# GEGLU feed-forward on one core: transposing x on TensorE in place of a transposing DMA, with warm-up matmuls and another order of the first loads

## The chip, the core and the metric

The kernel runs on one core of a Trainium2 chip. A core has a matrix engine (TensorE, PE in the profile, with its weight loads listed as PEld), a vector engine (VectorE, DVE), a scalar engine (ScalarE, ACT), GpSimd (POOL) and SyncE (SP), which here only issues transfers. Sixteen DMA engines move data between the main memory (HBM) and the on-chip memory (SBUF). Matmul results land in PSUM, 8 banks of 2 KB in each of 128 partitions. Each engine runs its own list of instructions; they meet at semaphores (`then_inc` raises one, `wait_ge` waits for it).

The metric is the device time of one execution in microseconds (us); the median of the runs counts.

## The reference

```python
B, S, D, F = 32, 32, 1024, 3584          # all bf16
x: (B, S, D)   w_gate, w_up: (D, F)   w_down: (F, D)

def reference(x, w_gate, w_up, w_down):
    return (gelu_tanh(x @ w_gate) * (x @ w_up)) @ w_down
```

With the tokens flattened, x is 1024 x 1024. The first two products are 1024 x 1024 x 3584 each, the third 1024 x 3584 x 1024. A matmul instruction takes 128 x 128 stationary weights and a moving tile of 128 x 512, so the products are 448 instructions each, 1344 in all.

## The kernel before

The contraction of the first two products runs over D, so both operands need D on the partitions. The weights have it so in memory; x has tokens there and must be transposed. The kernel keeps `xT` ([128, 8 chunks of D, 1024 tokens]) in SBUF for the whole run. P = 128, N = D = 1024, TT = DT = 8, TW = 512, TH = 2 halves of the tokens.

```python
    # F in 28 tiles of 128, loaded in groups: sizes 1, 1, 2, then 3 at a time
    NBUF_W = 3                      # weight buffers
    N_EARLY = min(2, NG)            # groups 0 and 1: GpSimd's queue
    N_ACTQ = 1 if NG > N_EARLY else 0   # group 2: ScalarE's queue
    ...
        def w_load(eng, g):         # two transfers, gate and up: rows of nft*128 bf16
            ...
        @block.sync
        def _(sp):
            for dc in range(DT):
                sp.dma_start(
                    out=xT[:, dc, :], in_=xf[:, dc * P : (dc + 1) * P], transpose=True
                ).then_inc(sem_x[dc], 16)
            wd_next = 0
            for g in range(N_EARLY + N_ACTQ, NG):
                slot = g % NBUF_W
                if g >= NBUF_W:
                    sp.wait_ge(sem_mm, last_job_of_group[g - NBUF_W] + 1)
                w_load(sp, g)
                ...                 # and one 1 MB piece of w_down
            ...                     # at the end: the stores of the output
        @block.gpsimd
        def _(pool):
            for g in range(N_EARLY):
                w_load(pool, g)
            ...                     # per job: hT = gu * sigmoid(z)
        @block.tensor
        def _(pe):
            for j, (g, ftl, th) in enumerate(jobs1):      # 56 jobs, 16 matmuls each
                slot = g % NBUF_W
                s = j % 4                                 # four pairs of PSUM banks
                bg = ps[:, 2 * s, 0:TW]
                bu = ps[:, 2 * s + 1, 0:TW]
                if ftl == 0 and th == 0:
                    pe.wait_ge(*w_wait[g])
                if j >= 4:
                    pe.wait_ge(sem_d1, j - 3)
                for wsb, bank in ((wg_sb, bg), (wu_sb, bu)):
                    for dc in range(DT):
                        if j == 0 and wsb is wg_sb:
                            pe.wait_ge(sem_x[dc], 16)
                        last = pe.matmul(bank, lhsT=wsb[...dc...], rhs=xT[:, dc, th * TW : (th + 1) * TW], ...)
                last.then_inc(sem_mm, 1)
            ...                                           # second loop: 16 jobs, 28 matmuls each
```

A job is one F tile for one half of the tokens. Groups 0 and 1 have two jobs each, group 2 has four. Per job ScalarE copies and squares the gate's bank, VectorE makes gate x up and the argument of the sigmoid, ScalarE the sigmoid and GpSimd the final product `hT`. The second loop multiplies `hT` with `w_down`; its results go through `o_sb` to memory.

## Time and profile before

| | us |
|---|---|
| time, median of 6 runs (lowest, highest) | 317.48 (317.3, 318.23) |
| span of the profiled execution | 315.8 |
| PE busy | 295.5 |
| DVE busy | 136.5 |
| ACT busy | 97.4 |
| POOL busy | 74.8 |
| PE idle before the first loop's matmuls, in all | 17.4 |

Times in the profile are microseconds from the start of the span; a line number such as L207 is a line of the kernel. Engine letters with a q (SPq) are the part of an engine that issues transfers. In a group of instructions, `out<-in` names the tensors written and read, and `x8` is how many instructions were merged. What stands in square brackets is the idle time before the instruction and what ended it. The chain of waits follows the work that ended last back to its start. A matmul's own listed duration (379 ns in the steady state) is longer than the distance from one to the next, because they are pipelined; the distance is what counts.

The profile lists these transfers in the first stage: eight transposing loads of x on SyncE's queue, two loads of 512 KB on ScalarE's queue (group 2), and four of 256 KB on GpSimd's (groups 0 and 1). The DMA engines moved 99 GB/s in the first 4 us, then 293, 212, 205 and 194 GB/s in the stages of 4 us up to 20 us.

### The profile page before, as it was taken

To read this page: it belongs to the slowest core of one execution; us is meant where nothing else is said; L and a number is where in the kernel's file an instruction comes from. 1 tells how busy PE (TensorE), PEld (TensorE's weight loads), DVE (VectorE), ACT (ScalarE), POOL (GpSimd) and SP (SyncE) were. 2 spreads that over 40 slices of the span, in tenths; PEclk is the share of its full clock that TensorE was granted. 3 is DMA by queue.
4 is the path that set the end of the run, shared out by engine and by line. 5 is a ranking of instruction groups with operands and counts; after the bars stand their busy time and mean duration, and the time that the engine had idled before them with its cause. 6 is when DMAs were issued, how large, how long until landed. Compare 5 with 4: busy or idle time off the path is not lost.

```text
span 315.8 us, 3313 instructions
## 1 busy us (share of the span) xinstructions
PE 295.5 (94%) x1344; PEld 132.1 (42%) x1344; DVE 136.5 (43%) x120; ACT 97.4 (31%) x178; POOL 74.8 (24%) x64
## 2 busy tenths in 40 slices
PE   0259999999999999999999999999999999999996
PEld 0014444444444444444444444444444444444442
DVE  0002566776676677667667766766000000000000
ACT  1003545445544544554454455444000000000000
POOL 4000433343343334334333433433000000000000
PEclk9999999999999999999999999999999999999999
DMA  7960994508118054090330000000010010001000
GB/s 194 211 126 5 352 309 134 199 3 264 68 47 289 0 173 161 0 312 22 91 110 0 2 0 0 2 0 0 17 35 17 17 35 17 17 17 35 17 17 33
DMA packets 33502, 26.41 MB, mean 84 GB/s; under 512 B 9168, under 2 KB 29648, under 8 KB 33488
## 3 DMA queue, kind: packets, MB, share of 16 engines
q1 hardware_dynamic: 31088, 24.12, 25.5%
q0 software_dynamic: 320, 1.05, 1.5%
q10 hardware_dynamic: 2080, 1.05, 1.3%
q8 instruction: 10, 0.16, 0.2%
q14 instruction: 4, 0.03, 0.0%
HBM read 22.02 MB, written 2.10 MB: 76 GB/s over the span
## 4 chain that ended last, share of the span: by engine, by line
PE 92%; SPq 5%; DMA 1%; DVE 0%; issue 0%
PE ps L207 62%; PE ps L230 31%; SPq L143 5%; DMA xT<-in_x_dram 1%; DVE o_sb L266 0%
## 5 line engine op out<-in xcount | busy, mean ns | idle before, releaser
L207 PE MATMUL ps<-xT,wg_sb 128*128 128x512 bf16 x448 | 109.5, 385 | 17.4 <-DMA wu_sb<-in_w_up_dram 12.0
L207 PE MATMUL ps<-xT,wu_sb 128*128 128x512 bf16 x448 | 107.6, 384 | 0.0
L183 POOL TENSOR_TENSOR hT<-gu_sb,s_sb 128x512 bf16<-128x512 f32 x56 | 70.9, 1267 | 145.9 <-ACT s_sb L295 145.9
L253 DVE SCALAR_TENSOR_TENSOR z_sb<-g_sb 128x512 f32<-128x512 f32 x56 | 97.1, 1733 | 0.0
L230 PE MATMUL ps<-wd_sb,hT 128*128 128x512 bf16 x448 | 96.9, 379 | 0.0
L248 DVE TENSOR_TENSOR gu_sb<-g_sb,ps 128x512 f32<-128x512 f32 x56 | 38.5, 688 | 88.9 <-ACT g_sb L286 88.9
L207 PEld LDWEIGHTS ps<-xT,wg_sb 128*128 128x128 bf16 x448 | 44.2, 99 | 73.6 <-DMA wu_sb<-in_w_up_dram 12.0
L283 ACT ACTIVATE g_sb<-ps 128x512 f32<-128x512 f32 x56 | 33.4, 597 | 124.1 <-PE ps L207 124.1
L207 PEld LDWEIGHTS ps<-xT,wu_sb 128*128 128x128 bf16 x448 | 44.2, 99 | 53.8 <-issue 1.9
L230 PEld LDWEIGHTS ps<-wd_sb,hT 128*128 128x128 bf16 x448 | 43.8, 98 | 52.9
L266 DVE CAST o_sb<-ps 128x512 bf16<-128x512 f32 x8 | 5.5, 692 | 88.4 <-PE ps L230 88.4
L295 ACT ACTIVATE s_sb<-z_sb 128x512 f32<-128x512 f32 x56 | 35.4, 632 | 1.9 <-DVE z_sb L253 1.9
L286 ACT ACTIVATE g_sb<-ps 128x512 f32<-128x512 f32 x56 | 33.1, 591 | 0.0
L310 ACT ACTIVATE o_sb<-ps 128x512 bf16<-128x512 f32 x8 | 4.8, 597 | 82.3 <-PE ps L230 82.3
L133 POOL DMA_DIRECT2D wg_sb<-in_w_gate_dram x2 | 1.9, 966 | 0.8 <-POOLq L328 0.8
L283 ACT ACT_TABLE_LOAD x1 | 1.3, 1283 | 1.8 <-issue 1.8
L136 POOL DMA_DIRECT2D wu_sb<-in_w_up_dram x2 | 1.8, 887 | 0.0
L295 ACT ACT_TABLE_LOAD x1 | 1.3, 1283 | 0.0
L328 POOL MEMSET const-float32-0.0<- 128x1 f32 x1 | 0.1, 99 | 0.2 <-issue 0.2
L328 POOL MEMSET const-bfloat16-1.0<- 128x1 bf16 x1 | 0.1, 102 | 0.0
L328 POOL MEMSET const-uint8-127<- 128x1 uint8 x1 | 0.1, 102 | 0.0
L328 POOL MEMSET const-float32-1.0<- 128x1 f32 x1 | 0.1, 99 | 0.0
## 6 DMA issues: line engine op xcount, KB each, us to landing
wd_sb<-in_w_down_dram SPq DMA_DIRECT2D x7, 1024.0 KB, 9.0
wg_sb<-in_w_gate_dram SPq DMA_DIRECT2D x8, 768.0 KB, 5.0
wu_sb<-in_w_up_dram SPq DMA_DIRECT2D x8, 768.0 KB, 6.9
out_dram<-o_sb SPq DMA_DIRECT2D x16, 128.0 KB, 1.7
wg_sb<-in_w_gate_dram ACTq DMA_DIRECT2D x1, 512.0 KB, 4.6
wu_sb<-in_w_up_dram ACTq DMA_DIRECT2D x1, 512.0 KB, 8.4
wg_sb<-in_w_gate_dram POOLq DMA_DIRECT2D x2, 256.0 KB, 9.2
wu_sb<-in_w_up_dram POOLq DMA_DIRECT2D x2, 256.0 KB, 9.6
```

The source lines that it names most:

```text
L133: eng.dma_start(out=wg_sb[:, slot, :, 0 : nft * P], in_=wg_v[:, :, fs * P : (fs + nft) * P]).then_inc(wsem, 16)
L143: sp.dma_start(out=xT[:, dc, :], in_=xf[:, dc * P : (dc + 1) * P], transpose=True).then_inc(sem_x[dc], 16)
L183: pool.tensor_tensor(out=hT[:, ft, th * TW : (th + 1) * TW], in0=gu_sb[:, k, :], in1=s_sb[:, k, :], op=ALU.mult,).then_inc(sem_h, 1)
L207: last = pe.matmul(bank, lhsT=wsb[:, slot, dc, ftl * P : (ftl + 1) * P], rhs=xT[:, dc, th * TW : (th + 1) * TW], start=(dc == 0), stop=(dc ...
L230: last = pe.matmul(bank, lhsT=hT[:, fc, tt * P : (tt + 1) * P], rhs=wd_sb[:, fc, dh * DW : (dh + 1) * DW], start=(fc == 0), stop=(fc == FT ...
L248: dve.tensor_tensor(out=gu_sb[:, k, :], in0=g_sb[:, k, :], in1=bu, op=ALU.mult).then_inc(sem_d1, 1)
L253: dve.scalar_tensor_tensor(out=z_sb[:, k, :], in0=g2_sb[:, k, :], scalar=GELU_A, in1=g_sb[:, k, :], op0=ALU.add, op1=ALU.mult,).then_inc(s ...
L266: dve.tensor_copy(out=o_sb[:, tt, dh * DW : (dh + 1) * DW], in_=ps[:, s2, 0:DW]).then_inc(sem_od, 1)
L283: act.activation(out=g_sb[:, k, :], in_=bg, func=ACT.Copy).then_inc(sem_a1, 1)
L286: act.activation(out=g2_sb[:, k, :], in_=bg, func=ACT.Square).then_inc(sem_a1, 1)
L295: act.activation(out=s_sb[:, k, :], in_=z_sb[:, k, :], func=ACT.Sigmoid, scale=GELU_C2).then_inc(sem_a2, 1)
L310: act.activation(out=o_sb[:, tt, dh * DW : (dh + 1) * DW], in_=ps[:, s2, 0:DW], func=ACT.Copy,).then_inc(sem_oa, 1)
```

## The change

The transposing loads are replaced. x is loaded as it lies in memory, in four transfers of two token tiles each (`x_nat`, rows of 2 KB). TensorE transposes it in 64 blocks of 128 x 128 with an identity matrix, eight blocks of one token tile into one PSUM bank; VectorE copies each bank to `xT`. The identity is made on GpSimd from a tile of ones. The output buffer `o_sb` now shares its memory with `x_nat`.

Two bursts of eight matmuls on a tile of ones, whose results nobody reads, are put ahead of the transposes and between token tiles 3 and 4; they are for the TensorE clock. The first weights change queues: group 0 is loaded by ScalarE, groups 1 and 2 by SyncE behind x, and GpSimd loads none. The first four jobs wait for copies to `xT` (a count, with a margin for the PSUM banks that the transposes used) where the first job waited for chunks of x.

```diff
-    N_EARLY = min(2, NG)
-    N_ACTQ = 1 if NG > N_EARLY else 0
+    N_POOLQ = min(2, NG)
+    N_ACTQ = 1 if NG > N_POOLQ else 0
+    N_STARTQ = N_POOLQ + N_ACTQ
 ...
+    XC = 2 if TT % 2 == 0 else 1
+    NXC = TT // XC
+    x_v = xf.rearrange("(tt p) d -> p tt d", p=P)
 ...
+        ones_sb = sb("ones", [P, P], BF16)
+        ident = sb("ident", [P, P], BF16)
+        x_nat = sb("x_nat", [P, TT, D], BF16)
+        o_sb = x_nat
 ...
         @block.sync
         def _(sp):
-            for dc in range(DT):
+            for c in range(NXC):
                 sp.dma_start(
-                    out=xT[:, dc, :], in_=xf[:, dc * P : (dc + 1) * P], transpose=True
-                ).then_inc(sem_x[dc], 16)
+                    out=x_nat[:, c * XC : (c + 1) * XC, :], in_=x_v[:, c * XC : (c + 1) * XC, :]
+                ).then_inc(sem_xc[c], 16)
+            w_load(sp, 1)
+            w_load(sp, 2)
 ...
         @block.gpsimd
         def _(pool):
-            for g in range(N_EARLY):
-                w_load(pool, g)
+            pool.memset(ones_sb[:], 1.0).then_inc(sem_ident, 1)
+            pool.wait_ge(sem_ident, 1)
+            pool.affine_select(out=ident[:], in_=ones_sb[:], ...).then_inc(sem_ident, 1)
 ...
         @block.tensor
         def _(pe):
+            def warm(n):
+                for _ in range(n):
+                    pe.matmul(ps[:, 7, 0:TW], lhsT=hT[:, 0, 0:P], rhs=hT[:, 0, 0:TW],
+                              start=True, stop=True)
+
+            pe.wait_ge(sem_wm, 1)
+            warm(8)
+            pe.wait_ge(sem_ident, 2)
+            for tt in range(TT):
+                if tt == 4:
+                    warm(8)
+                if tt % XC == 0:
+                    pe.wait_ge(sem_xc[tt // XC], 16)
+                bank_bf = ps[:, tt, :].bitcast(BF16)
+                ins = None
+                for dc in range(DT):
+                    ins = pe.transpose(
+                        out=bank_bf[:, dc * P : (dc + 1) * P],
+                        in_=x_nat[:, tt, dc * P : (dc + 1) * P],
+                        identity=ident[:],
+                    )
+                ins.then_inc(sem_tp, 1)
             for j, (g, ftl, th) in enumerate(jobs1):
 ...
-                if j >= 4:
+                if j < 4:
+                    pe.wait_ge(sem_xT, min(TT, max(2 * s + 2, (th + 1) * TPW)))
+                else:
                     pe.wait_ge(sem_d1, j - 3)
 ...
-                        if j == 0 and wsb is wg_sb:
-                            pe.wait_ge(sem_x[dc], 16)
 ...
         @block.vector
         def _(dve):
+            dve.memset(hT[:, 0, 0:TW], 1.0).then_inc(sem_wm, 1)
+            for tt in range(TT):
+                dve.wait_ge(sem_tp, tt + 1)
+                bank_bf = ps[:, tt, :].bitcast(BF16)
+                dve.tensor_copy(
+                    out=xT[:, :, tt * P : (tt + 1) * P],
+                    in_=bank_bf[:, 0 : DT * P].rearrange("p (dc t) -> p dc t", dc=DT),
+                ).then_inc(sem_xT, 1)
 ...
         @block.scalar
         def _(act):
-            for g in range(N_EARLY, N_EARLY + N_ACTQ):
-                assert g < NBUF_W
-                w_load(act, g)
+            w_load(act, 0)
```

## The prediction

> **What bounds the kernel now.** I read the page from the top: busy time, then the chain that ended last, and then went to the stage that the chain points at. The busy row and the head of the chain:

> ```profile
> PE 295.5 (94%) x1344; PEld 132.1 (42%) x1344; DVE 136.5 (43%) x120; ACT 97.4 (31%) x178; POOL 74.8 (24%) x64
> ...
> PE ps L207 62%; PE ps L230 31%; SPq L143 5%; DMA xT<-in_x_dram 1%; DVE o_sb L266 0%
> ```

> TensorE (PE) is the bound: 93% of the chain is its two matmul loops. The rest is almost all one thing: 5% is SyncE's queue issuing the eight transposing loads of x (line 143), 1% the last of these landing. The chain in order of time says where that lies:

> ```profile
> 13.92 1.30 SPq L143
> 15.22 0.04 issue
> 15.26 1.30 SPq L143
> 16.56 0.04 issue
> 16.60 1.30 SPq L143
> 17.90 0.04 issue
> 17.94 3.71 DMA xT<-in_x_dram
> 21.65 0.05 issue
> 21.70 194.58 PE ps L207 x889
> 216.28 96.71 PE ps L230 x448
> 312.98 0.02 issue
> 313.01 0.69 DVE o_sb L266
> ```

> Columns: start, length, what. From 21.70 us to 312.98 us the PE never waits. Before 21.70 it does next to nothing: of 896 matmuls in the first loop 889 lie after it, so seven ran before. The second loop gives the steady pace: 96.71/448 = 0.216 us per matmul. 889 of these would be 191.9 us, the chain has 194.58, so some 2.7 us were lost to something at the start. The timeline shows it:

> ```profile
> 12.03 0.61 PE L207 MATMUL ps<-xT,wg_sb 128*128 128x512 bf16 x1 [12.03 <-DMA wu_sb<-in_w_up_dram]
> ...
> 22.10 3.62 PE L207 MATMUL ps<-xT,wu_sb 128*128 128x512 bf16 x8
> ...
> 22.10 0.15 PEld L207 LDWEIGHTS ps<-xT,wu_sb 128*128 128x128 bf16 x1 [0.28 <-issue]
> 22.52 0.15 PEld L207 LDWEIGHTS ps<-xT,wu_sb 128*128 128x128 bf16 x1 [0.28 <-issue]
> ```

> Weight loads start 0.42 us apart up to about 26.8 us: the first dozen matmuls of the unbroken stream run at half pace, 12 x 0.21 = 2.5 us. So I set an **effective start**: the moment from which 1344 matmuls at 0.216 us would end where they do. It is 21.70 + 2.7 - 7 x 0.216 = 22.9 us. Everything that the change can win is in this number; the loops after it are untouched.

> What fills the first 22 us is DMA. Asked for that window alone, the queues are:

> ```profile
> q1 hardware_dynamic: 8448, 2.10, 53.9%
> q0 software_dynamic: 320, 1.05, 21.3%
> q10 hardware_dynamic: 2080, 1.05, 18.7%
> ```

> Columns: packets, MB, share of 16 engines over 22 us. q1 is x: 8192 of its packets carry 256 bytes, and 0.539 x 22 x 16 / 8448 = 22.5 ns each. q10 is group 2's weights, 512-byte rows, 0.187 x 22 x 16 / 2080 = 31.6 ns each. The engines are simply full from 3 to 20 us, and more than half of their time goes to the 2 MB of x in small pieces.

> [...] 0.42 us per matmul, then 0.216, some 5 us after the stream became dense. [...] the three shares add to 94%.

> **The change part by part.**

> *Removed: the transposing loads.* Eight loads in 256-byte pieces, 8448 x 22.5 ns / 16 = 11.9 us of all engines. *Added: four plain loads of x* in 2 KB rows. At 32 to 40 us the kernel before loads 768-byte and 2 KB rows at 345 and 367 GB/s (stages of 4 us); 2.10 MB at 350 GB/s is 6.0 us.

> *Moved: the first weights.* Group 0 (0.52 MB, 2048 rows of 256 bytes) goes from GpSimd's queue to ScalarE's, groups 1 and 2 go behind x on SyncE's. Taking 22.5 ns for a 256-byte packet, group 0 is 2048 x 22.5 / 16 = 2.9 us. In 4 to 8 us the engines moved 293 GB/s in a mixture; 2.62 MB (x and group 0) at that rate is 8.9 us, which fits 6.0 + 2.9. Data began to flow at about 2.5 us, so I set the last piece of x and group 0 at 11 to 12 us, pieces landing every 2.1 us from about 5.

> *Added: two bursts of 8 dummy matmuls, 64 transposes and 8 copies.* The first burst, 8 x 0.42 = 3.4 us from about 1.3 us, lies before x is there: free. The transposes have no measured row here. With a 128-column stream they should take a quarter of a matmul, 0.11 us at half pace, and the weight load of 0.10 to 0.15 us may rule instead; I take 0.12, so 0.96 us a token tile and 1.9 us for the two tiles of a load. That keeps up with 2.1 us per load. What is certainly on the path is the last load's two tiles: 1.9 us after 11 to 11.5. The second burst (1.7 us at full pace, 3.4 at half) sits between tiles 3 and 4; tiles 0 to 3 can be done at about 9, so it ends at 10.7 to 12.4, and half of it may be on the path. [...] VectorE follows the PE, and job 0 needs only the first four tiles; the last copy has all of job 0 (16 matmuls, 3.5 us) to end in. The hot loop's instructions are the same.

> *Sum.* Job 0 starts at about 11.3 + 1.9 = 13.2, plus some 0.5 for the burst: 13.7 us. The half-pace loss is 2.5 us if the gate is shut again and 0 if the burst has opened it; I take 0.8. Effective start 14.5 in place of 22.9: 8.4 us less, 317.5 - 8.4 = 309.1 us. Later weights: group 1 (0.52 MB) is due at job 2, 7 us after the start, at 20.7, and 1.5 MB behind x at 260 GB/s is through by about 18; group 2 is due at 27. So no new wait.

> **The rivals.**

> *The PE becomes the bound of the start.* If the gate stays shut through the transposes [...], the first tiles end at 9.5, the burst at 12.9, tiles 4 to 7 at 0.12 to 0.15 us per transpose at 16.8 to 17.7, and job 0 then still loses 2.5 us. Effective start about 19.5: 314 us, a gain of 1%. For it: in the trace before, matmuls scattered over 12 to 21 us did not open the gate; the dense stream needed 5 us more. Against it: a burst of dense matmuls right ahead of the work is there to do just that.

> *The weights come last.* [...] then half of group 0 is left when x is done and shares the engines with group 1. It would land at 13.5 to 14.5, with the transposes long done: effective start 14.5 to 16, 309 to 311 us. For it: in the trace before, it was weights that ended the first wait, at 12.03 us. This rival costs little against my main line, since it lies beside the transposes.

> *All goes well.* x in by 10, the burst hidden, the gate open: job 0 at 11.8 at full pace, 306.4 us.

> *No gain* would need a wait of 8 us that I can't find: copies, identity (two GpSimd instructions while x is in flight) and the output are small or hidden.

> **Range and chances.** The sum lies at 309.1; the good case 306.4, the late weights up to 311, the shut gate 314. A few tenths for the late case leave the middle at 309.3. The range is 306.3 to 312.8. Faster by over 2% means below 311.1 us, an effective start before 16.5: only the shut gate in most of its extent misses that. I give it 0.76, within 2% 0.23, slower 0.01.

> **What would show it.** In the changed profile: x landing between 5 and 12 us with about 1024 packets; job 0's first matmul at 12.5 to 15 us and no idle PE after it; the chain's head being the last x load or group 0's weights, then transposes, and no line of SyncE's transposing issue; the second loop still 0.216 us per matmul; weight loads 0.22 us apart soon after job 0 starts. I'm wrong if the PE is busy with transposes and bursts right up to a start after 16 us, if a dozen matmuls of job 0 are 0.43 us apart, if PE waits at job 1 for copies or at job 2 for group 1, or if something inside the loops has slowed.

## The result, and the profile after

The changed kernel takes 307.01 us (median of 8 runs, 306.75 to 307.29) where the kernel before took 317.35 us beside it: a ratio of 0.9669, 95% interval 0.9656 to 0.9682. That is 3.3% faster. The prediction was 309.3 us with a range of 306.3 to 312.8.

Busy time and the head of the chain in the changed kernel. Lines have moved: L254 and L277 are the two matmul loops, L165 the loads of x, L220 the dummies, L234 the transposes, L292 the copies to `xT`.

```profile
PE 299.1 (98%) x1424; PEld 136.8 (45%) x1424; DVE 142.1 (47%) x129; ACT 97.4 (32%) x178; POOL 71.7 (24%) x62
...
PE ps L254 63%; PE ps L277 32%; DMA x_nat<-in_x_dram 3%; SPq L165 0%; PE ps L234 0%; DVE x_nat L321 0%
```

SyncE's issuing, 5% of the chain before, is gone; 3% now is one wait for the plain loads of x. The chain in order of time (start, length, what):

```profile
2.30 8.67 DMA x_nat<-in_x_dram
10.97 0.04 issue
11.01 1.07 PE ps L234 x16
12.08 193.39 PE ps L254 x896
205.47 96.71 PE ps L277 x448
302.18 0.02 issue
302.20 0.69 DVE x_nat L321
```

The last load of x lands at 10.97 us, its sixteen transposes take 1.07 us, and from 12.08 us on all 1344 matmuls run without a gap. 193.39/896 = 0.216 us: full pace from the first. The effective start is therefore 12.08 us in place of 22.9, and the 10.8 us between them are the whole difference of the two spans (315.8 and 305.0). The second loop still takes 96.71 us, to the last digit what it took before.

The same stage in the timeline:

```profile
4.76 1.05 PE L234 MATMUL ps<-ident,x_nat 128*128 128x128 bf16 x16
7.16 1.07 PE L234 MATMUL ps<-ident,x_nat 128*128 128x128 bf16 x16 [1.35 <-DMA x_nat<-in_x_dram]
8.07 1.89 PE L220 MATMUL ps<-hT 128*128 128x512 bf16 x8
9.79 1.06 PE L234 MATMUL ps<-ident,x_nat 128*128 128x128 bf16 x16
11.01 1.07 PE L234 MATMUL ps<-ident,x_nat 128*128 128x128 bf16 x16 [0.16 <-DMA x_nat<-in_x_dram]
11.92 1.89 PE L254 MATMUL ps<-xT,wg_sb 128*128 128x512 bf16 x8
```

Read the square brackets: the transposes wait for x, 1.35 us and 0.16 us, and job 0 follows the last of them without a pause. From one transpose to the next are 0.056 us; the 1.07 us of sixteen have the length of the last one in them. The second burst of dummies, 8.07 to about 9.8 us, lies almost wholly in the wait for the third load, which landed at 9.44 us.

And the DMA queues of the first 22 us (packets, MB, share of 16 engines):

```profile
q1 hardware_dynamic: 5845, 4.13, 70.5%
q10 hardware_dynamic: 2080, 0.52, 10.9%
```

4.67 MB in that time where the kernel before moved 4.20, in 7926 packets rather than 10848. And their order differs: x and group 0 come first. That this matters more than the form of x is what the experiments show.

### The profile page after: what moved, and what is told of

Its sections match the earlier page's. It is cut to its first block, busy times and chain, and to the rows that moved or that the text cites. A ratio compares the mean times of both kernels' runs of the same rounds, so it can differ in the third digit from the quotient of the medians.

```text
span 305.0 us, 3483 instructions
## 1 busy us (share of the span) xinstructions
PE 299.1 (98%) x1424; PEld 136.8 (45%) x1424; DVE 142.1 (47%) x129; ACT 97.4 (32%) x178; POOL 71.7 (24%) x62
## 3 DMA queue, kind: packets, MB, share of 16 engines
q10 hardware_dynamic: 2080, 0.52, 0.8%
## 4 chain that ended last, share of the span: by engine, by line
PE 95%; DMA 3%; SPq 0%; DVE 0%; issue 0%
PE ps L254 63%; PE ps L277 32%; DMA x_nat<-in_x_dram 3%; SPq L165 0%; PE ps L234 0%; DVE x_nat L321 0%
## 5 line engine op out<-in xcount | busy, mean ns | idle before, releaser
L254 PE MATMUL ps<-xT,wu_sb 128*128 128x512 bf16 x448 | 105.8, 379 | 0.0
L254 PE MATMUL ps<-xT,wg_sb 128*128 128x512 bf16 x448 | 105.8, 379 | 0.0
L277 PE MATMUL ps<-wd_sb,hT 128*128 128x512 bf16 x448 | 96.9, 379 | 0.0
L254 PEld LDWEIGHTS ps<-xT,wu_sb 128*128 128x128 bf16 x448 | 43.8, 98 | 52.9
L277 PEld LDWEIGHTS ps<-wd_sb,hT 128*128 128x128 bf16 x448 | 43.8, 98 | 52.9
L254 PEld LDWEIGHTS ps<-xT,wg_sb 128*128 128x128 bf16 x448 | 43.8, 98 | 52.6
L321 DVE CAST x_nat<-ps 128x512 bf16<-128x512 f32 x8 | 5.5, 692 | 88.4 <-PE ps L277 88.4
L363 ACT ACTIVATE x_nat<-ps 128x512 bf16<-128x512 f32 x8 | 4.8, 597 | 82.3 <-PE ps L277 82.3
L292 DVE COPY xT<-ps 128x1024 bf16<-128x1024 bf16 x8 | 5.1, 686 | 6.4 <-PE ps L234 6.4
L220 PE MATMUL ps<-hT 128*128 128x512 bf16 x16 | 5.1, 478 | 1.5 <-DVE hT L288 1.5
L234 PE MATMUL ps<-ident,x_nat 128*128 128x128 bf16 x64 | 4.2, 219 | 1.5 <-DMA x_nat<-in_x_dram 1.5
L234 PEld LDWEIGHTS ps<-ident,x_nat 128*128 128x128 bf16 x64 | 3.7, 98 | 2.6 <-DMA x_nat<-in_x_dram 1.9
L220 PEld LDWEIGHTS ps<-hT 128*128 128x128 bf16 x16 | 1.8, 119 | 3.9 <-issue 1.7
```

Of the source, the lines that this page charges most:

```text
L220: pe.matmul(ps[:, 7, 0:TW], lhsT=hT[:, 0, 0:P], rhs=hT[:, 0, 0:TW], start=True, stop=True)
L234: ins = pe.transpose(out=bank_bf[:, dc * P : (dc + 1) * P], in_=x_nat[:, tt, dc * P : (dc + 1) * P], identity=ident[:],)
L254: last = pe.matmul(bank, lhsT=wsb[:, slot, dc, ftl * P : (ftl + 1) * P], rhs=xT[:, dc, th * TW : (th + 1) * TW], start=(dc == 0), stop=(dc ...
L277: last = pe.matmul(bank, lhsT=hT[:, fc, tt * P : (tt + 1) * P], rhs=wd_sb[:, fc, dh * DW : (dh + 1) * DW], start=(fc == 0), stop=(fc == FT ...
L292: dve.tensor_copy(out=xT[:, :, tt * P : (tt + 1) * P], in_=bank_bf[:, 0 : DT * P].rearrange("p (dc t) -> p dc t", dc=DT),).then_inc(sem_xT, 1)
L321: dve.tensor_copy(out=o_sb[:, tt, dh * DW : (dh + 1) * DW], in_=ps[:, s2, 0:DW]).then_inc(sem_od, 1)
```

## The experiments

All times are medians, each beside runs of the kernel before on the same chip. The effective start is reckoned from the one profiled execution of each kernel: the span, less 2.8 us after the last matmul, less 1344 x 0.216 us. Four of these executions lie off their median: 317.30 us (kernel before with dummies, first try), 307.91 us (first burst only), 307.35 us (second burst only) and 308.03 us (start on half of x).

| kernel | us | kernel before beside it | effective start |
|---|---|---|---|
| new order of weights alone (x still transposed by DMA) | 311.01 | 317.98 | 16.4 |
| the same with dummies | 309.10 | 317.87 | 14.3 |
| changed kernel | 307.10 | 317.87 | 12.3 (12.1 in the profile above) |
| changed kernel, old order of weights | 312.43 | 317.98 | 17.7 |
| kernel before with dummies, first try | 316.07 | 317.67 | 22.6 |
| kernel before with dummies, gaps closed | 316.05 | 317.98 | 21.5 |
| changed kernel without dummies | 308.15 | 317.67 | 13.2 |
| first burst only | 307.02 | 317.67 | 13.1 |
| second burst only | 307.76 | 317.67 | 12.5 |
| start on half of x | 307.55 | 317.98 | 13.1 |
| start on half of x, jobs reordered | 306.60 | 317.87 | 11.8 |
| x in eight loads | 307.24 | 317.87 | 12.4 |

**Two theories.** Mine was: the engines' time ahead of job 0 falls because x comes in large pieces and groups 1 and 2 come later, in shares that my sum did not part; and the dummies bring TensorE to full pace. The rivals: it is the order of the weights that frees the engines, not the form of x; and the transposes themselves bring it there. "The gate" stands for this change of pace, as in the prediction: shut is half pace, 0.42 to 0.43 us from one weight load to the next (kernel before, 22.1 to 26.8 us), open is full pace, 0.216 us (96.71/448 in the second loop).

### Without the dummies

```diff
-            pe.wait_ge(sem_wm, 1)
-            warm(8)
 ...
-                if tt == 4:
-                    warm(8)
```

> The changed kernel without its sixteen dummy matmuls. If the dummies open the clock gate [...]: transposes at about 0.13 us in place of 0.067, job 0 starts at 12 to 13 us and its first dozen matmuls are 0.43 us apart, so about 309.5 to 311 us. Rival, transposes alone open the gate: job 0 at full pace, 307 us, or slightly less as the second burst leaves the path.

308.15 us (306.90 to 308.27; ratio 0.9681, interval 0.9647 to 0.9715). The PE's timeline:

```profile
4.77 1.86 PE L230 MATMUL ps<-ident,x_nat 128*128 128x128 bf16 x16 [4.77 <-DMA x_nat<-in_x_dram]
...
9.47 3.60 PE L230 MATMUL ps<-ident,x_nat 128*128 128x128 bf16 x32 [0.49 <-DMA x_nat<-in_x_dram]
13.19 1.67 PE L250 MATMUL ps<-xT,wg_sb 128*128 128x512 bf16 x7
14.70 1.89 PE L250 MATMUL ps<-xT,wu_sb 128*128 128x512 bf16 x8
```

The transposes run at half pace, 0.107 us from one to the next, but job 0 starts at full pace: 14.70 - 13.19 is 1.51 us for the seven matmuls listed (one record is missing), 0.216 each. So something opened the gate before job 0, and only transposes had run. Without dummies the start costs 1.1 us more in this profile, all of it in slower transposes: the last load of x landed at 10.90 us, and the transposes went on to 13.06. To that extent the PE did become the bound of the start. One of the four runs took only 306.9.

### First burst only

```diff
-                if tt == 4:
-                    warm(8)
```

> The changed kernel with the eight dummies at the start, without those between tiles 3 and 4. If one burst opens the gate and the gaps of 1 to 3 us while x arrives do not close it: 307 us, the second burst lies wholly in the wait for x. Rival, the gate closes again: half pace in job 0, 308.5 to 309.5 us.

307.02 us (306.81 to 307.95; ratio 0.9664, interval 0.964 to 0.9688). Four runs lie at 306.8 to 307.1 and two at 307.9; the profile is one of the two. Its busy time by stage (stage, length, PE busy, PEld, DVE, ACT, POOL, granted clock, DMA share, GB/s):

```profile
7.10:8.20 1.10, 1.01 (x16) 0.83 (x16) 0.69 (x2) 0.00 (x0) 0.00 (x0) 1.00 1.09 337
8.20:9.50 1.30, 0.04 (x1) 0.05 (x2) 0.79 (x2) 0.00 (x0) 0.00 (x0) 1.00 1.08 366
9.50:11.00 1.50, 1.50 (x16) 1.50 (x17) 0.53 (x1) 0.00 (x0) 0.00 (x0) 0.52 1.19 297
11.00:12.00 1.00, 1.00 (x12) 1.00 (x11) 0.84 (x2) 0.00 (x0) 0.00 (x0) 0.50 1.35 219
12.00:13.00 1.00, 0.99 (x10) 0.94 (x9) 0.70 (x2) 0.00 (x0) 0.00 (x0) 0.51 1.25 235
13.00:14.00 1.00, 0.90 (x5) 0.42 (x5) 0.69 (x1) 0.00 (x0) 0.00 (x0) 1.00 1.19 291
```

The clock column settles it. After a gap of 1.35 us the clock falls to half (0.52), stays there for 3.4 us in which the PE does nothing but 32 transposes, and is full again (1.00) as they end. With nothing but these transposes the clock came back from half to 1.00. The mean granted clock of the other runs fits: 0.994 in both runs of 307.9 us, 1.000 in the four shorter ones. The second burst is thus an insurance: it fills the gap in which the gate closed in two of these six runs, which cost about 1 us each time (307.9 us in place of 306.8 to 307.1).

The gap alone does not decide. The changed kernel has one of 1.35 us too (before 7.16 us) and keeps its clock. In these three traces the changes of the clock lie 3.41 us apart, or twice that: at 6.15, 9.57 and 12.98 us in this run, at 4.67, 11.50 and 18.32 us in the kernel before with dummies (first try), at 7.03, 10.44 and 13.86 us in the changed kernel with the old order of weights. In the last 3.41 us before the fall in each the PE was busy for 1.59, 1.17 and 1.09 us. In the changed kernel the clock is full from 4.21 us, and in the 3.41 us after that, which hold its gap, the PE was busy for 2.03 us. The steps begin elsewhere in each execution (4.21 us there and 6.15 us here, after the same burst from 1.52 us).

### Second burst only

```diff
-            pe.wait_ge(sem_wm, 1)
-            warm(8)
 ...
                 if tt == 4:
+                    pe.wait_ge(sem_wm, 1)
                     warm(8)
```

> The changed kernel with only the dummies between tiles 3 and 4. If a burst must come early: it runs at half pace, 3.4 us in place of 1.9, so tiles 4 to 7 end about 1.5 to 3 us later and part of job 0 is at half pace, 309 to 311 us. Rival, the second burst alone is enough: 307 to 308.5 us.

307.76 us (307.28 to 308.62; ratio 0.9683, interval 0.9659 to 0.9707).

```profile
7.10 1.85 PE L233 MATMUL ps<-ident,x_nat 128*128 128x128 bf16 x16 [0.47 <-DMA x_nat<-in_x_dram]
8.79 1.89 PE L220 MATMUL ps<-hT 128*128 128x512 bf16 x8
```

The first 32 transposes run at half pace (1.86 and 1.85 us for sixteen), the burst already at full (1.89 us for eight): these transposes had opened the gate. In the 3.41 us up to there, 8.78 us, the PE was busy for 2.94 us, with transposes alone. The rival holds. Together the bursts are worth some 1 us at most, and not in every run.

### The kernel before, with dummies

```diff
+            pe.wait_ge(sem_wm, 1)
+            warm(28)
 ...
+                        if j == 0 and wsb is wg_sb and dc < DT - 1:
+                            warm(4)
```

> The kernel before, its transposing loads and queues kept, with 28 dummies at the start and 4 after each of the first seven matmuls of job 0, to keep the gate open while x lands. If the effective start is the landing of x plus a loss of 2.7 us to the gate, as I reckoned: that loss goes and no more, 314.6 to 315.2 us. Rival, the gate is no large part of the gain: 317 us.

316.07 us (314.68 to 317.55; ratio 0.9956, interval 0.9941 to 0.9971). A miss. The gate closed while the PE idled up to 14 us (granted clock 0.52 from 14 to 18.5 us), and I took this for the reason, since four dummies at half pace, 1.7 us, are longer than the 1.3 us between landings of x. But from 18.5 us on the dummies ran at full pace, and what job 0 waited for at the end was x: its last chunk landed at 23.73 us, where the kernel before had it at 21.65 us, and the matmul on it began 0.17 us later.

```diff
-            warm(28)
+            warm(40)
 ...
-                            warm(4)
+                            warm(3)
```

> As the run with bursts in the kernel before, with 40 dummies at the start (they end at about 12 us, where group 0 lands) and 3 between the matmuls of job 0, so that the PE has no gap and the dummies fit between the landings of x. If the earlier run fell short because the gate closed in the gap of 4.75 us and dummies at half pace then stood in the path: now 314.8 us, the whole 2.7 us. Rival, the loss can't be had back that way: 316 us.

316.05 us (315.58 to 318.05; ratio 0.9952, interval 0.992 to 0.9983).

```profile
22.77 0.39 PE L215 MATMUL ps<-xT,wg_sb 128*128 128x512 bf16 x1
23.00 1.89 PE L215 MATMUL ps<-xT,wu_sb 128*128 128x512 bf16 x8
```

The stream of job 0 is now at full pace once x is there, and the effective start is 21.5 us: the half pace is gone. That the gain is 1.9 us and not 2.7 is x again: its last chunk landed at 22.73 us, 1.1 us later than in the profile of the kernel before, after the dummies ahead of it had run. The gate is not the reason. The clock did fall to 0.50 between 16 and 18 us in this profile, but three of the six runs kept a mean granted clock of 1.000 and took 315.86 to 316.45 us, against 315.58 to 318.05 in the other three. The gate's share in the kernel before is real. Why x landed later in both profiles with dummies stays open; runs of the kernel before alone spread from 316.57 to 319.41 us here.

### Only the order of the weights

```diff
+            w_load(sp, 1)
+            w_load(sp, 2)
 ...
-            for g in range(N_EARLY):
-                w_load(pool, g)
 ...
-            for g in range(N_EARLY, N_EARLY + N_ACTQ):
-                assert g < NBUF_W
-                w_load(act, g)
+            w_load(act, 0)
```

> The kernel before with only the new order of the first weights: group 0 on ScalarE's queue, groups 1 and 2 behind x on SyncE's. x is still transposed by the DMA. If the engines' time is the bound of the start: x (190 us of engine time) and group 0 (some 46) on 16 engines end 14.8 us after 2.5, so x lands at about 17.3 in place of 21.7 and the time is about 313 us, with the half-pace loss still there. Rival, the order of the weights is worth nothing: 317.5 us.

311.01 us (310.46 to 311.93; ratio 0.9795, interval 0.9767 to 0.9824): 6.5 of the 10.8 us of effective start, with not one transpose on TensorE. The chain in order of time:

```profile
11.38 3.57 DMA xT<-in_x_dram
14.95 0.05 issue
14.99 11.62 PE ps L207 x42
```

x lands at 14.95 us in place of 21.65. Its packets are as small as ever; what went is the competition of 1.57 MB of weights that nobody needs before job 2 (groups 1 and 2) and that all shared the 16 engines with x (the three queues filled 53.9, 21.3 and 18.7% of them in the first 22 us of the kernel before). x landed earlier than the 17.3 us that I expected. A likely reason is that more than one packet is in flight on an engine (DMA share 1.34 from 4 to 6 us), so that adding packet times overstates the engines' time.

Two things are not parted from the order by any run. Groups 0 and 1 also left GpSimd's queue, which is of another kind (`software_dynamic`); but group 0 is no cheaper on ScalarE's: its 0.52 MB fill the 16 engines for 10.9% of 24 us, 2.6 us, where the 1.05 MB on GpSimd's filled them for 21.3% of 22 us, 4.7 us. And SyncE's issuing of the eight loads got shorter with them (kernel before, then this run):

```profile
0.75 18.49 SPq L143 DMA_TRANSPOSE xT<-in_x_dram  x8
0.74 12.14 SPq L143 DMA_TRANSPOSE xT<-in_x_dram  x8
```

No transposing load took SyncE less than 1.23 us to issue. Once the competition is gone, this issuing may bound the start as much as the DMA engines do.

### Everything but the order of the weights

```diff
-            w_load(sp, 1)
-            w_load(sp, 2)
 ...
+            w_load(pool, 0)
+            w_load(pool, 1)
 ...
-            w_load(act, 0)
+            w_load(act, 2)
```

> The changed kernel with the weights on the old queues: groups 0 and 1 on GpSimd's, group 2 on ScalarE's, so all three compete with x. If the order of the weights is part of the gain: 4.2 MB at about 300 GB/s, x lands at 14 to 16.5 us, job 0 starts at 14.5 to 17.5: 309.5 to 312 us. Rival, plain rows of x are the whole gain: 307 us.

312.43 us (312.13 to 312.65; ratio 0.9834, interval 0.9807 to 0.9861).

```profile
2.31 14.23 DMA x_nat<-in_x_dram
16.55 0.04 issue
16.59 1.07 PE ps L234 x16
```

With three queues at work the last plain load of x lands 5.6 us later than in the changed kernel. This kernel has its dummies too, so its 5.6 us over the kernel before are not the form of x alone. Four kernels with dummies part the two: they gain 1.9 us (neither, gaps closed), 5.6 (plain loads), 8.8 (new order; the next run) and 10.8 us (both). So the order wins 6.8 us without and 5.2 us with the plain loads, the plain loads with the transposes on TensorE 3.6 and 2.0. Both work on the DMA time ahead of job 0. Together they win 1.6 us less than one by one, which is within the noise of the four intervals.

### The order of the weights and dummies

```diff
 (as in the run with only the new order, and)
+            pe.wait_ge(sem_wm, 1)
+            warm(15)
 ...
+                        if j == 0 and wsb is wg_sb and dc < DT - 1:
+                            warm(3 if dc < DT - 2 else 1)
```

> The kernel before with the new order of the weights and dummies (15 at the start, 3 or 1 between the matmuls of job 0): all of the change except the way x is transposed. If order of weights and gate are independent terms: x at 15.0 us, no half pace, effective start 13.7 to 14.5: 308.5 to 309.5 us, so that the transposes on TensorE are worth 1.5 to 2.5 us beside them. Rival, dummies stand in the path or the gate stays shut: 311 us.

309.10 us (308.69 to 309.30; ratio 0.9718, interval 0.9695 to 0.9741), effective start 14.3 us, as expected.

```profile
11.52 3.71 DMA xT<-in_x_dram
15.23 0.05 issue
15.28 1.90 PE ps L215 x8
```

x lands at 15.23 us, and what follows runs at full pace. The changed kernel in the same group is 2.0 us faster.

### Starting on half of x

```diff
+        jobs1 = [(0, 0, 0), (1, 0, 0), (0, 0, 1), (1, 0, 1)]
 ...
+            sp.dma_start(out=wg_sb[:, 0, :, 0:P], in_=wg_v[:, :, 0:P]).then_inc(sem_ws[0], 16)
+            x_load(0)
+            x_load(1)
+            sp.dma_start(out=wu_sb[:, 0, :, 0:P], in_=wu_v[:, :, 0:P]).then_inc(sem_wu0, 16)
             w_load(sp, 1)
+            x_load(2)
+            x_load(3)
             w_load(sp, 2)
 ...
-            warm(8)
+            warm(10)
 ...
-                if tt == 4:
-                    warm(8)
 ...
+                    if j == 1 and wsb is wu_sb:
+                        tp(4)
+                        tp(5)
 ...
+                if j == 1:
+                    tp(6)
+                    tp(7)
```

`tp` transposes one token tile, `x_load` loads two; from group 2 on the jobs are as before. The second burst is left out, and the first has ten dummies.

> The changed kernel, starting on half of x: one queue carries, in this order, group 0's gate, tiles 0 to 3 of x, group 0's up, group 1, tiles 4 to 7, group 2; jobs 0 and 1 are both of the first half of the tokens, and tiles 4 to 7 are transposed inside and after job 1. If the start is bound by the bytes ahead of the first job: job 0 starts at about 8 in place of 12.1 us, about 1 us is lost at job 2 to the last copies, 304 us. Rival, later weights or copies take it back: 306 to 307 us with PE waits at jobs 1 to 4.

307.55 us (307.50 to 308.03; ratio 0.9687, interval 0.9664 to 0.971): no gain over the changed kernel. The first matmuls of jobs 0 and 2:

```profile
10.03 1.67 PE L271 MATMUL ps<-xT,wg_sb 128*128 128x512 bf16 x7 [1.03 <-DVE xT L312]
20.05 1.67 PE L271 MATMUL ps<-xT,wg_sb 128*128 128x512 bf16 x7 [1.16 <-DVE xT L312]
```

Job 0 started at 10.03 us, not 8: tiles 2 and 3 landed at 7.89 us, and the copies of the last two tiles, hidden under tiles 4 to 7 in the changed kernel, now stood before it (1.03 us), and again before job 2 (1.16 us). And the 32 later transposes, 0.89 us for sixteen (15.37 to 16.27 us in this run's chain), moved into the stream; the PE has to run them in either place. What could be won at all was the waiting for x, 1.35 + 0.16 us, and the burst's 1.7.

```diff
-        jobs1 = [(0, 0, 0), (1, 0, 0), (0, 0, 1), (1, 0, 1)]
+        jobs1 = [(0, 0, 0), (1, 0, 0), (2, 0, 0), (0, 0, 1), (1, 0, 1), (2, 0, 1)]
 ...
-                    if g >= 2:
+                    if g > 2 or (g == 2 and ftl > 0):
```

> As the start on half of x, with group 2's first tile for the first half of the tokens as job 2, so that the copies of tiles 6 and 7 lie beside it. If the wait of 1.16 us at job 2 was what the half start lost against the changed kernel: about 306.4 us, and no wait at job 2. Rival, group 2's weights end that wait in its place: 307.5 us.

306.60 us (306.04 to 306.83; ratio 0.9639, interval 0.9615 to 0.9662). The PE's waits for copies (in total, times, longest):

```profile
PE ps L271 <- DVE xT L312: 1.0, 1, 1.0
```

The one left is ahead of job 0; the wait at job 2 is gone. Against the changed kernel in the same group (307.10, 306.99 to 307.23) it is 0.5 us less; the runs don't overlap, the intervals of the two ratios do.

### Loads of one tile, and the changed kernel once more

```diff
-    XC = 2 if TT % 2 == 0 else 1
+    XC = 1
```

> The changed kernel with x in eight loads of one token tile. If the last load's two tiles of transposes (1.07 us) are the tail of the start: half of it goes, 306.5 us. Rival, group 0's weights, which landed at 11.4 us, or slower small loads take it back: 307 us.

> The changed kernel once more, beside the runs of this group, for the direct comparison: 307.0 us.

307.24 us (306.94 to 307.31; ratio 0.966, interval 0.9637 to 0.9682) against 307.10 (ratio 0.9657, interval 0.9635 to 0.9679): no gain. The chain:

```profile
8.22 0.62 PE ps L234 x8
8.84 1.73 PE ps L220 x8
10.57 1.79 PE ps L234 x32
```

Tile 3 landed at 8.18 us, where the two-tile load had brought it at 7.12: to that extent the small loads were slower, as the rival had it. After 8.2 us no load of x ends a wait (the last landed at 10.99 us), and group 0 was there at 7.5 us. The second burst (L220, 1.73 us), free in the changed kernel, is now itself on the path, and the gain expected at the tail has nothing to come from.

## Why the prediction was right, step by step

The direction, the stage and the bound were right: all of the gain lies before job 0, both loops run as before, no new wait came at jobs 1 to 4, and the time lies in the range. The reckoned effective start was 14.5 us, the measured one 12.1. The terms of the sum:

- *x and group 0 have landed at 11 to 12 us* (11.3 in the sum): x at 10.97; group 0's second half at 11.4, issued at 1.33 and 10.1 us on its way (the line below). Right, 0.3 us too late. Some luck may be in it: a sum of that kind, by packet times alone, was 2.3 us too late for x in the run with only the new order of weights.
- *1.9 us for the last load's two tiles*: 1.07. The transposes were mis-sized, 0.12 us each where they came 0.056 us apart with the gate open (and 0.107 with it shut, which is about what I had assumed).
- *0.5 us for the second burst*: 0, since it lay in the wait for the third load.
- *0.8 us for half pace*: 0. Job 0 began at full pace.
- *The copies to `xT`*: 0.686 us each (the second line below), the last from 12.3 us on, inside job 0 as expected. No row of the profile before is a copy of this form; the nearest, VectorE's copies of 128x512 fp32 out of PSUM to bf16 (L266), took 692 ns each.

```profile
wu_sb<-in_w_up_dram ACTq DMA_DIRECT2D x1, 256.0 KB, 10.1
L292 DVE COPY xT<-ps 128x1024 bf16<-128x1024 bf16 x8 | 5.1, 686 | 6.4 <-PE ps L234 6.4
```

0.3 + 0.8 + 0.5 + 0.8 is 2.4 us, all of the difference. All four terms erred to the same side; the range was wide enough to hold that.

What the prediction had wrong was a reason. It put the gate's opening down to the burst and feared that the gate stays shut through the transposes, which no trace had shown; the rival "the PE becomes the bound of the start" (314 us) rests on that, and the runs with a burst left out show the reverse: the gate opens on transposes alone (by 8.8 us with the second burst only, as that burst began), and without any dummies the PE as the bound costs 1.1 us, not 5. Had I weighed only what the trace before showed, the shut gate would have counted for less in the odds.

And it didn't part the gain. Adding the parts one after another, the order of the weights gives 22.9 - 16.4 = 6.5 us, an open gate 2.1 and the transposes on TensorE 2.2. Added in another order the shares come out differently; only the first row of the table tells what the order wins alone. The rival "the weights come last" (13.5 to 14.5 us) did not come about: group 0 landed at 11.4 us, 0.5 us ahead of its use. That half of group 0 would be left when x is done was the author's estimate; how the engines divide their time between the two queues no run here shows. More of x was moved at the end, as its last three loads (1.57 MB) landed between 7.1 and 11 us and the other half of group 0 (0.26 MB) only at 11.4.

Open: why the gate closed in two of six runs with only the first burst and not in four. The steps of 3.41 us, which begin elsewhere in each execution, are a likely reason, since the same gaps then fall into one step or into two; but only one of the six was profiled, and what the clock does between the 1.59 us of work after which it fell and the 2.03 us after which it stayed no run measured.

## What to carry to other kernels

Before the first matmul of a kernel, count what shares the DMA engines with the operands that it waits for: weights due 7 us later, in other queues, cost more here (5.2 to 6.8 us) than the small pieces of a transposing load (2.0 to 3.6). Queue later loads behind the first ones on the same queue. And before work is moved out of a start-up phase, look at whether it fills a wait there: work in a wait was free here (the second burst, almost wholly in the wait for the third load), moved into the stream it was not (0.89 us for sixteen transposes in the start on half of x), and when the wait went, its filler came onto the path (1.73 us of dummies in the run with eight loads).
